# Attention with normalized q and k, then a hard-swish feed-forward: a longer planned time for transposing DMAs and a fourth staging buffer

## The chip, the cores and the metric

The kernel runs on one core of a Trainium2 chip. Such a core has five engines, each of which takes its own list of instructions strictly in order: TensorE (PE in the profile; its weight loads are shown apart as PEld), VectorE (DVE), ScalarE (ACT), GpSimd (POOL) and SyncE (SP). They wait for each other through semaphores. SP here issues nearly all the DMAs; GpSimd issues those that load the weights.

The metric is the time of one execution on the device in microseconds. The kernel before took 441.98 us, the median of three runs (438.52, 443.76 and 441.98).

## What is computed

Eight sequences of 448 rows with 12 heads of 64 go through attention; q and k are normalized by their root mean square first. The output is laid out as 3584 rows of 768 and goes through a feed-forward block with 2048 inner columns.

```python
def rmsnorm(x, g):
    return x / np.sqrt(np.mean(x * x, axis=-1, keepdims=True) + 1e-06) * g
q_n, k_n = rmsnorm(q, g_q), rmsnorm(k, g_k)
scores = np.matmul(q_n, k_n.transpose(0, 1, 3, 2)) / np.sqrt(64)
attn = softmax(scores)                       # over the last axis
x = np.matmul(attn, v).transpose(0, 2, 1, 3).reshape(8 * 448, 768)
h = x @ w_in
out = (h * np.clip(h + 3.0, 0.0, 6.0) / 6.0) @ w_out
```

Inputs and output are float32; the kernel multiplies in bfloat16.

## The kernel before

**Tiling.** Two heads make a pair (`p`, 48 of them counted from 0, six per sequence); two pairs make a group (24), which is the unit of loading. The 448 rows of a head are three tiles of 128 and a rest of 64; the rests of two heads share a tile.

**Steps of a pair.** k, q and v of a group are loaded by SP into one of `NS` staging buffers (`kq_in`, `v_st`: L235, L236; `load_k` L287, `load_q` L278, `load_v` L294). Per pair, GpSimd (early also ScalarE) squares q and k (L334, L332), VectorE sums the squares (L337), ScalarE makes the reciprocal root (L345, L348), and GpSimd multiplies (L353), which gives `qk`, still with rows on the partitions. `qk` is then transposed. For the first 14 pairs (`TD`) TensorE does it (L367), with copies out of its accumulator by VectorE or ScalarE (L385, L388, called at L303). From pair 14 on a transposing DMA on SP does it in one step (`transposes_dma`, L377: 128 rows of 1024 bfloat16), and ScalarE multiplies the q half by the gains afterwards (`scale_q`, L374). Then come the scores on TensorE (L395, for the rests L402), the exponential on ScalarE (L408), the weighting of v on TensorE (L429, L435), and the division on VectorE (L445, L446), which gives `xn`. A second transpose brings `xn` into `xT`: on TensorE for the first 12 pairs (`XD`; L464, L475), after that by another transposing DMA on SP (L468).

**Feed-forward.** For each sequence and each of 16 inner tiles six matmuls (L479) read `xT`; ScalarE and VectorE form the gate (L485, L490) into `gT`; then rows of the output are 16 matmuls of 384 columns each (L498), copied out (L303) and stored by SP (L510). These matmuls fill TensorE between the steps of attention, and about the last 100 us are nothing else.

**What sets the order.** No order is written out by hand. When the program is built, class `Plan` plays it through: each operation has a key (lower goes first), one or several engines with a duration, the operations that it depends on, and a `lag`, the time from the end of its issue to its result. `Plan.run` goes forward in planned time and gives each engine that is free the ready operation with the lowest key. The order in which it hands them out becomes the order of each engine's instructions. On the chip the semaphores see to it that data is there; so a planned time that is too short gives no wrong result, but an instruction that stands in its engine's list before its data has come, with everything behind it waiting too.

For a transposing DMA, `dma_transpose` plans 1270 ns on SP and a lag. Both kinds use it: q and k with `transposes_dma`, `xn` with `x_out_dma` (in `x_stage`). A plain load is planned with 600 ns for each issue on SP and a lag of 1700 ns (`ISSUE`, `LAND`), and all DMAs share one planned pipe of 270 bytes per ns.

**Buffers.** A load into a staging buffer depends on the work that read it before: for k and q the two normalizations of the group `NS` groups earlier, for v its casts. These lines say it (L680, L681); `g` is the group, `norm_g` its normalizations, `vc` the casts of v:

```python
old = norm_g[g - NS] if g >= NS else [clr[g]]
oldv = vc[p - NS * GP:p - NS * GP + GP] if g >= NS else [clv[g]]
```

Each staging buffer is cleared once where the rests leave rows empty (`clear`, `clear_v`: L518 to L524). Other rings keep their sizes: four of `kq`, three of `qk` and `xn`, eight of exponentials, two of squares and of sums.

**Weights.** GpSimd issues the weight loads (L313, L318) between its own work, released in the plan after the v loads of given groups.

Of the kernel before, what the change touches and what calls it, by code (L numbers as in the profile page):

```python
# [63 lines left out]
class Plan:  # L64
# [28 lines left out]
        return op  # L93

    def dma_transpose(self, key, size, fn, deps):
        return self.add(key, [("SP", 1270, fn)], deps, 2100, 1.4 * size)

    def item(self, lane, place, count, ns, fn, deps):

# [89 lines left out]
def kernel(  # L189
# [22 lines left out]
    NFT = DFF // P  # L212
    assert D == 64 and NT == 3 and REST == 64 and DM == H * D and B % 2 == 0

    NS = 3
    GP = 2
    NV, NK, NX, NE, NQ = 4, 4, 3, 8, 3
    YC = 384
# [8 lines left out]
    def ring(n, shape, dtype, name, pool=const):  # L227
        return [pool.tile(shape, dtype, name=f"{name}{i}") for i in range(n)]
# [5 lines left out]
    gprime = const.tile([P, 1], FP32, name="gprime")  # L234
    kq_in = ring(NS, [P, GP, 2, 2, 4, D], FP32, "kq_in")  # L235
    v_st = ring(NS, [P, GP, 2, 4, D], FP32, "v_st")  # L236
    vaug = ring(NV, [P, 4, 2, D + 1], BF16, "vaug")
# [34 lines left out]
    def part_of(p, n):  # L272
        return (p // GP) % NS, slice(p % GP, p % GP + n)

# [30 lines left out]
    def cast(eng, out, in_):  # L305
        if eng is nc.vector:
            eng.tensor_reduce(out=out, in_=in_.unsqueeze(len(in_.shape)), axis=mybir.AxisListType.X, op=A_MAX)
        else:
            copy(eng, out=out, in_=in_)
# [12 lines left out]
    def which(part):  # L322

        return slice(0, 2) if part == 2 else slice(part, part + 1)

    def raw(p, part):
        return kq_in[(p // GP) % NS][:, p % GP, :, which(part)].rearrange("p h a t d -> p h (a t) d")

# [30 lines left out]
    def cast_v(eng, p):  # L359
        out = vaug[p % NV][:, :, :, 0:D].rearrange("p t h d -> p h t d")  # L360
        in_ = v_st[(p // GP) % NS][:, p % GP]
        cast(eng, out, in_)
# [153 lines left out]
    def clear(eng, i):  # L516

        eng.memset(kq_in[i][REST:P, :, 0, 0, NT, :], 0.0)  # L518
        eng.memset(kq_in[i][0:REST, :, 1, 0, NT, :], 0.0)
        eng.memset(kq_in[i][REST:P, :, :, 1, NT, :], 0.0)  # L520

    def clear_v(eng, i):
        eng.memset(v_st[i][REST:P, :, 0, NT, :], 0.0)
        eng.memset(v_st[i][0:REST, :, 1, NT, :], 0.0)  # L524
# [136 lines left out]
    def by(key, pool, dve, fn, deps):  # L661
        return add(key, [("POOL", pool, lambda: fn(G)), ("DVE", dve, lambda: fn(V))], deps)
# [4 lines left out]
    clear_v(V, 0)  # L667
    clr = [by((i * GP - 3, 0), 600, 350, lambda e, i=i: clear(e, i), []) if i else None for i in range(NS)]
    clv = [by((i * GP - 3, 1), 350, 200, lambda e, i=i: clear_v(e, i), []) if i else None for i in range(NS)]
# [168 lines left out]
```

## Time and profile before

| | |
|---|---|
| median of 3 runs | 441.98 us (438.52 to 443.76) |
| the profiled execution | 439.38 us, of which the span in the trace is 437.6 |
| PE busy | 409.8 us, 94% |
| DVE / ACT / POOL busy | 234.7 / 254.3 / 195.2 us |
| DMA | 64.55 MB, 148 GB/s over the span |
| granted TensorE clock | 0.996 of full speed |

The page also gives the busy share in 40 slices of the span, 10.9 us each, in tenths (9 is 90% or more), and the busy share of the 16 DMA engines in the same way:

```profile
PE   0677899999999998999999999999999999999997
ACT  3886887734877885968778587666643032132100
POOL 3697785596377776859676556311000000000000
DMA  6999999995978898999999994333211201100022
```

TensorE is filled after the first five slices up to the end, with one slice at 8 in the middle. The DMA engines are full for most of the first 24 slices, which is where q, k, v and the weights are loaded, and where the transposing DMAs run; GpSimd ends with them. Afterwards only feed-forward work is left.

How such lines are read: in a list of waits, "DVE rden L445 <- PE av L435: 47.1, 45, 3.4" means that VectorE stood idle before its instructions of line 445 (which write `rden`) until TensorE had ended those of line 435, 47.1 us in sum, 45 times, 3.4 at the longest. In a timeline the columns are start, duration, engine, line, operation, out<-in with shapes, count, and in brackets the idle time before it with what ended it. A matmul's bar is longer than the time by which it holds up the next one, since matmuls are pipelined.

### The profile page before, as it was taken

Reading aid. Unit: us, or ns where it says so; the run is one execution under the profiler, and the core shown is the slowest. Engines: PE = TensorE matmul, PEld = TensorE weight load, DVE = VectorE, ACT = ScalarE, POOL = GpSimd, SP = SyncE. Lnnn points to the kernel's source line nnn. Section 1 sums busy time; section 2 is a strip of 40 time slices with the busy share of each in tenths; the row PEclk is TensorE's granted clock in tenths of the full one; section 3 lists DMA queues with packets and bytes.
Section 4 is the critical chain, followed back from the end, with each engine's and each line's share of the span. In section 5 each row is a group of like instructions: output and inputs, shape, how many; then the busy total and the mean of one; then the engine's idle time right before and its main releaser. Section 6 shows DMA issues by size and latency. Waiting matters only on the chain.

```text
span 437.6 us, 8944 instructions
## 1 busy us (share of the span) xinstructions
PE 409.8 (94%) x3520; PEld 236.5 (54%) x3520; DVE 234.7 (54%) x492; ACT 254.3 (58%) x414; POOL 195.2 (45%) x146
## 2 busy tenths in 40 slices
PE   0677899999999998999999999999999999999997
PEld 0355565555566554555555555555565555555565
DVE  6486777766455557556466366344444253343322
ACT  3886887734877885968778587666643032132100
POOL 3697785596377776859676556311000000000000
PEclk9998999999999999999999999999999999999999
DMA  6999999995978898999999994333211201100022
GB/s 170 267 228 216 221 222 239 250 190 131 237 161 190 204 217 189 201 219 194 227 212 167 191 213 121 73 88 91 61 24 49 72 1 51 59 36 37 25 85 73
DMA packets 126506, 64.55 MB, mean 148 GB/s; under 512 B 77824, under 2 KB 123008, under 8 KB 126464
## 3 DMA queue, kind: packets, MB, share of 16 engines
q1 hardware_dynamic: 117488, 57.24, 57.5%
q0 software_dynamic: 8144, 6.29, 9.2%
q8 instruction: 27, 0.44, 0.4%
q10 hardware_dynamic: 832, 0.46, 0.4%
q14 instruction: 15, 0.12, 0.1%
HBM read 45.61 MB, written 11.01 MB: 129 GB/s over the span
## 4 chain that ended last, share of the span: by engine, by line
PE 82%; DMA 7%; ACT 3%; DVE 3%; SPq 2%; POOL 2%; issue 1%; ACTq 0%; POOLq 0%
PE m L479 18%; PE m L498 17%; PE t_ps L498 9%; PE t_ps L479 8%; PE av L435 7%; PE sc L395 6%; PE sc L498 6%; PE sc L479 4%; DMA kq_in<-in_k_dram 3%; DMA kq<-qk 3%; PE av L429 2%; DMA kq_in<-in_q_dram 2%; PE sc L402 2%; ACT eT L408 2%; DVE ssq L337 1%
## 5 line engine op out<-in xcount | busy, mean ns | idle before, releaser
L408 ACT ACTIVATE eT<-sc 128x896 bf16<-128x896 f32 x168 | 147.2, 915 | 42.2 <-PE sc L395 38.5
L498 PEld LDWEIGHTS <-gT 128*128 128x128 bf16 x912 | 85.5, 98 | 61.7 <-issue 8.9
L479 PE MATMUL m<-xT,w_in_sb 128*128 128x448 bf16 x486 | 109.9, 353 | 1.7 <-DVE xT L475 0.6
L479 PEld LDWEIGHTS <-w_in_sb 128*128 128x128 bf16 x768 | 70.7, 98 | 68.8 <-issue 12.0
L353 POOL TENSOR_TENSOR qk<-kq_in,rstd 128x1024 bf16<-128x1024 f32 x47 | 89.0, 1903 | 41.6 <-DMA kq<-qk 20.8
L498 PE MATMUL m<-w_out_sb,gT 128*128 128x384 bf16 (+1 forms) x480 | 87.3, 324 | 0.0
L334 POOL TENSOR_TENSOR sq<-kq_in 128x1024 f32<-128x1024 f32 x41 | 77.2, 1894 | 13.0 <-DMA kq_in<-in_q_dram 3.6
L490 DVE SCALAR_TENSOR_TENSOR gT<-t_sb,m 128x448 bf16<-128x448 f32 x81 | 49.9, 618 | 41.8 <-ACT t_sb L485 41.4
L485 ACT ACTIVATE t_sb<-m 128x448 f32<-128x448 f32 x81 | 44.1, 546 | 47.9 <-PE m L479 47.2
L337 DVE TENSOR_REDUCE ssq<-sq 128x16 f32<-128x1024 f32 (+1 forms) x49 | 58.1, 1190 | 9.5 <-POOL sq L334 7.5
L435 PE MATMUL av<-vaug,eT 128*128 128x65 bf16 x1152 | 59.6, 196 | 0.0
L435 PEld LDWEIGHTS <-eT 128*128 128x128 bf16 x1152 | 52.8, 100 | 7.2 <-issue 1.6
L498 PE MATMUL t_ps<-w_out_sb,gT 128*128 128x384 bf16 x256 | 46.9, 326 | 0.0
L395 PE MATMUL sc<-kq 64*128 64x448 bf16 x288 | 41.6, 363 | 4.0 <-ACT eT L408 2.5
L429 PE MATMUL av<-vaug,eT 128*128 128x130 bf16 x192 | 43.0, 224 | 2.4 <-ACT eT L408 1.2
L479 PE MATMUL t_ps<-xT,w_in_sb 128*128 128x448 bf16 x192 | 44.5, 352 | 0.7 <-DVE gT L490 0.7
L303 POOL CAST vaug<-v_st 128x512 bf16<-128x512 f32 x33 | 20.3, 620 | 55.0 <-PE av L435 46.6
L445 DVE RECIPROCAL rden<-av 128x4 f32<-128x4 f32 x96 | 17.3, 180 | 48.8 <-PE av L435 47.1
L446 DVE TENSOR_TENSOR xn<-av,rden 128x256 bf16<-128x256 f32 x96 | 40.7, 424 | 3.3
L374 ACT ACTIVATE kq<-kq,gprime 128x448 bf16<-128x448 bf16 x34 | 22.8, 670 | 14.2 <-DMA kq<-qk 14.2
L498 PE MATMUL sc<-w_out_sb,gT 128*128 128x384 bf16 (+1 forms) x176 | 29.1, 319 | 0.0
L485 ACT ACTIVATE t_sb<-t_ps 128x448 f32<-128x448 f32 x32 | 17.5, 547 | 19.7 <-PE t_ps L479 18.5
(50 smaller groups left out, 225.0 us busy)
## 6 DMA issues: line engine op xcount, KB each, us to landing
v_st<-in_v_dram SPq DMA_DIRECT2D x24, 384.0 KB, 4.7
kq_in<-in_k_dram SPq DMA_DIRECT2D x23, 384.0 KB, 4.5
kq_in<-in_q_dram SPq DMA_DIRECT2D x23, 384.0 KB, 4.8
out_dram<-y_sb SPq DMA_DIRECT2D x23, 384.0 KB, 2.6
w_out_sb<-in_moe_w_out_dram POOLq DMA_DIRECT2D x4, 768.0 KB, 19.1
w_in_sb<-in_moe_w_in_dram POOLq DMA_DIRECT2D x3, 768.0 KB, 16.2
out_dram<-y_sb SPq DMA_DIRECT2D x9, 192.0 KB, 2.7
v_st<-in_v_dram SPq DMA_DIRECT2D x48, 32.0 KB, 4.3
```

Of the source, the lines that this page charges most:

```text
L334: eng.tensor_tensor(out=sq, in0=x, in1=x, op=A_MULT)
L337: nc.vector.tensor_reduce(out=ssq_r[(p // GP) % 2][:, p % GP, :, which(part)].rearrange("p h a t -> p h (a t)"), in_=sq_r[m][:, :, which(p ...
L353: eng.tensor_tensor(out=qk_r[p % NQ][:].rearrange("p a t h d -> p h (a t) d"), in0=raw(p, 2), in1=rstd_r[(p // GP) % 2][:, p % GP].rearran ...
L395: nc.tensor.matmul(out=sc[:, h, 0:S], lhsT=kT_r[p % NK][rows, t * P:(t + 1) * P], rhs=qT_r[p % NK][rows], start=True, stop=True,)
L408: nc.scalar.activation(out=e2_r[d % NE][:, :, 0:S], in_=sc_r[i][:, :, 0:S], func=EXP, bias=0.0, scale=1.0,)
L429: nc.tensor.matmul(out=av, lhsT=rest[:, cols], rhs=va[:, 3].rearrange("p h d -> p (h d)"), start=True, stop=False, skip_group_check=True,)
L435: nc.tensor.matmul(out=av[:, h * W:(h + 1) * W], lhsT=e[t][h][:, cols], rhs=va[:, t, h], start=False, stop=(t == NT - 1 and h == 1), skip_ ...
L446: nc.vector.tensor_tensor(out=xn_r[p % NQ][:, t].rearrange("p n (h d) -> p n h d", h=2), in0=av4[:, :, :, 0:D], in1=rden.unsqueeze(3).to_b ...
L479: nc.tensor.matmul(out=m[:, 0:S], lhsT=w_in_sb[:, kt, f * P:(f + 1) * P], rhs=xT[:, kt, b % NX, x_slot(b)], start=(kt == 0), stop=(kt == N ...
L485: nc.scalar.activation(out=t[:], in_=m[:, 0:S], func=RELU, bias=0.5, scale=1.0 / 6.0,)
L490: nc.vector.scalar_tensor_tensor(out=gT[:, f, (b % 2) * S:(b % 2 + 1) * S], in0=t[:], scalar=1.0, in1=m[:, 0:S], op0=A_MIN, op1=A_MULT,)
L498: nc.tensor.matmul(out=m[:, 0:n], lhsT=gT[:, f, c0:c0 + P], rhs=w_out_sb[:, f, c:c + n], start=(f == 0), stop=(f == NFT - 1),)
```

## The change

Two numbers change. The lag of both kinds of transposing DMAs in the plan goes from 2100 to 3500 ns; the planned time on SP stays at 1270. The number of staging buffers for groups goes from three to four, for `kq_in` and for `v_st`.

```diff
     def dma_transpose(self, key, size, fn, deps):
-        return self.add(key, [("SP", 1270, fn)], deps, 2100, 1.4 * size)
+        return self.add(key, [("SP", 1270, fn)], deps, 3500, 1.4 * size)
```

```diff
-    NS = 3
+    NS = 4
     GP = 2
```

No operation is computed differently. There are five more clears for the fourth buffer. Because both numbers enter the plan, the order of instructions changes on every engine, and some operations that may run on several engines (casts, copies, squares) go to another one.

## The prediction

> **What bounds the kernel now.** I read four views in this order: busy time by stretch of the span, the chain of waits (for the pace of TensorE), who waited for whom, and the timelines of ScalarE and TensorE around the longest of those waits.
>
> ```profile
> core 0: us, PE busy (x) PEld busy (x) DVE busy (x) ACT busy (x) POOL busy (x), PEclk, DMA share, GB/s
> 20.00:60.00 40.00, 33.64 (x401) 21.72 (x400) 29.98 (x70) 31.35 (x50) 33.87 (x26) 0.96 1.13 224
> 60.00:150.00 90.00, 89.94 (x820) 52.02 (x819) 56.67 (x113) 60.95 (x101) 61.39 (x40) 1.00 0.94 201
> 150.00:240.00 90.00, 85.91 (x806) 48.52 (x804) 57.26 (x112) 69.13 (x117) 64.48 (x41) 1.00 0.97 203
> 240.00:310.00 70.00, 70.00 (x646) 39.18 (x644) 34.11 (x77) 49.55 (x77) 25.56 (x19) 1.00 0.62 127
> ```
>
> TensorE (PE) is the bound: outside the start its bars fill every stretch but 150 to 240, where 4.1 us are open. A bar is longer than a matmul's share of PE, so open time is understated. The pace comes from the chain of waits:
>
> ```profile
> 377.26 2.60 PE m L498 x16
> 382.46 1.13 PE t_ps L479 x6
> 154.83 0.48 PE sc L395 x4
> 155.80 0.06 PE av L429
> 155.86 0.19 PE av L435 x6
> ```
>
> That is 0.1625 us for L498, 0.189 for L479 (and L402, as wide), 0.12 for L395, 0.06 for L429 and 0.032 for L435 (the small transposes L367 and L464, by the same view, 0.055). With the counts of matmuls by line, the work in 150 to 240 is 141 x 0.1625 + 175 x 0.189 + 14 x 0.189 + 84 x 0.12 + 56 x 0.06 + 336 x 0.032 = 82.8 us, so 7.2 us of 90 went unused. The same sum leaves 1.9 unused in 60 to 150, 1.3 in 240 to 310, 0.9 after 310, 13.3 in 20 to 60 and 17.3 in 0 to 20. All work is the same after the change, so only these can shrink or grow. What stands behind the 7.2:
>
> ```profile
> ACT kq L374 <- DMA kq<-qk: 14.2, 11, 2.8
> PE sc L402 <- ACT eT L408: 2.0, 3, 0.9
> PE sc L395 <- ACT eT L408: 1.5, 2, 1.0
> PE t_ps L479 <- DVE gT L490: 0.7, 1, 0.7
> ```
>
> ```profile
> 170.23 0.67 ACT L374 ACTIVATE kq<-kq,gprime 128x448 bf16<-128x448 bf16 x1 [2.82 <-DMA kq<-qk]
> 170.80 1.71 ACT L408 ACTIVATE eT<-sc 128x896 bf16<-128x896 f32 x2
> 171.75 0.36 PE L395 MATMUL sc<-kq 64*128 64x448 bf16 x2 [1.04 <-ACT eT L408]
> 175.80 0.54 PE L402 MATMUL sc<-kq 128*128 128x448 bf16 x2 [0.76 <-ACT eT L408]
> ```
>
> ScalarE takes its work in the planned order. The planner puts the scaling of q (L374) where it believes the transposing DMA (L377) to be done, 1.27 + 2.1 = 3.37 us after its issue begins. The DMA is later, ScalarE stands 2.82 us, and the exponentials queued behind it (L408, of the pairs before) come late; they hold the score buffers, so PE stands at the next scores. How late the DMA is (issue to landing, in 150 to 250 us):
>
> ```profile
> DMA to landing us min/median/max: 3.1/4.1/6.0
> ```
>
> **The change, part by part.**
>
> *The longer planned time.* Planned landing goes from 3.37 to 4.77 us after issue; no instruction is added. The eleven waits of L374 are 0.81, 2.82, 0.95, 1.12, 1.30, 1.47, 0.41, 1.98, 1.77, 0.91 and 0.62 us. With 1.4 us taken off each, 1.42 + 0.07 + 0.58 + 0.37 = 2.4 of 14.2 are left, so 83% go. The new order agrees: between a scaling and the first exponential of its own scores there stood 4.4 exponentials on average, now 3.3, and for pairs 22 to 29 (scores from about 155 to 200 us) two to five fewer. One exponential is 0.915 us, so the shift is about the 1.4 us. Of the 7.2 us unused I leave 1.9 as the floor that the 90 us before show; 5.3 are stalls, 4.4 of them the five waits for L408 (3.5 idle, and about 0.16 each under the tail of a bar, 0.353 long against 0.189) and 0.9 the gate (L490). Gain: 4.4 x 0.83 = 3.7 us.
>
> Is something else late next? What is placed later on ScalarE is also later on PE: from the eighth group of heads on, scores stand 2 to 5 us of PE work later in the new order (78.5 to 82.7 us of work ahead of them, at the end 276.2 to 280.4), with feed-forward matmuls drawn ahead in their place. The last 100 us of PE work are the same in both orders. Attention ends later with no cost while the first feed-forward matmul of the last batch (at 312.3 us of PE work in both) still finds its input: the last weighting ends at 296.8, and division, transposing DMA and landing take about 0.6 + 4.7 us from their longest rows, so 10 us of cover remain; without it each us would cost one.
>
> By the Trainium skill, page "DMA: Bandwidth & Descriptors", section "Anatomy of one DMA — SWDGE (gpsimd) path", a DMA is about 2.0 us and bytes over 436 GB/s; for the 262 KB of this one that makes an estimated 2.6 us, the old plan would already be long enough and this term zero. The trace disagrees (3.1 at the least, 4.1 median), so the row decides.
>
> *The fourth staging buffer.* It lets loads run further ahead on SP's queue. Counted in the order, the load of a group's k stood 3 to 5 pairs ahead of its own transpose from the eleventh to the sixteenth group, now 6; squares on GpSimd (L334) stood 0 to 2 pairs ahead of their normalization, now mostly 3. That removes the 0.9 us of the gate: the chain there goes back over ssq and sq (161.16) to a load of k that took 3.50 us from 157.09. SP issues as many transfers as before, the loads about one group earlier; so the first transposing DMA of q and k (91.25 us now) has one more group's k and q ahead of it. These two loads take about 4 us (0.92 MB at 224 GB/s); the scores behind that DMA start at 108.5 now and 4.2 us of work later then, so 10 us of cover stay.
>
> *The start.* PE's order is the same up to 12 us of work (36.4 us of span). The fifth group's k and q now go ahead of its v: 0.46 MB less ahead of them. ScalarE waits 0.74 us for that q (square at 32.11) and PE stands 0.53 us on the exponential behind it: gain 0.7. On GpSimd the squares of the sixth group move ahead of the fifth group's normalization:
>
> ```profile
> 44.98 3.76 POOL L353 TENSOR_TENSOR qk<-kq_in,rstd 128x1024 bf16<-128x1024 f32 x2 [0.45 <-ACT rstd L348]
> 48.70 3.74 POOL L334 TENSOR_TENSOR sq<-kq_in 128x1024 f32<-128x1024 f32 x2
> 55.62 3.76 POOL L353 TENSOR_TENSOR qk<-kq_in,rstd 128x1024 bf16<-128x1024 f32 x2
> ```
>
> GpSimd is free for them from 39.1 (a square from 37.25); the second needs a sum that VectorE ends at 42.58, so it ends at 44.5, and the normalization at 44.98 starts no later. The next one can then follow at 50.2 instead of 55.62, and its transpose stands 5.9 us of work earlier on PE (28.9 to 23.0; PE is at 23.0 at 52.42): just in time. The gate that waited for the sum of the square at 48.70 (0.5 us idle on PE and 0.1 under a bar) comes free: gain 0.6. From below: all this fails if the sixth group's k and q land late. They are issued by 34.9 and used at 48.70; 1.9 us earlier, they land between 37.8 (median landing 4.8) and 46.8. At the late end the squares end at 50.6, the normalization waits from 44.98 to 50.6, and PE loses 5.6. Earlier loads of the first four groups keep their order, so nothing better than 3 us is in reach (the gaps over 0.3 us from 30 to 50 sum to 5). I take 1.3, near the early end: the fifth group's q, issued by 28.5, was used at 32.11, so a load there took less than the median.
>
> *Five more clears* on VectorE, ahead of its first sum (starts 6.29; the clears end at 5.42 and five take 1.1 more): 0.3 us late, hidden behind the q load that lands at 13.9; 0.3 without that cover. Casts move between engines (VectorE three rows more, ScalarE four fewer), all under 80% busy: nothing.
>
> Sum: 3.7 + 0.9 + 1.3 = 5.9 us. The profiled execution took 439.38 (span 437.6 and 1.8 around it): 433.5. Against the median of 441.98 it is 2.6 short, so on the median 436.1; I say 436.
>
> **The rivals.**
> 1. *The start pays it back.* The late end above: minus 4.6, plus 5.6, 443. For it, the DMA share is 1.13 there and SP takes 4.77 us over one load from 36.97; against it, the order of issue. 15%.
> 2. *The reckoning was not what held ScalarE*, so waits only move: the landing is 3.1 where ScalarE waits and something else comes last. Only gate and start are left, 2.2 us: 440. The skill's fit above would give this. Eleven waits ending at the landing speak against it. 8%.
> 3. *Slower: transposes land later still.* Deeper loads on the same queue stand ahead of each transpose, and in the new order 9 of 34 scalings stand with no exponential between them and their own scores, against 3. Waits of 14.2 cost 5.3 us, 0.37 each. A median landing m costs 34 x (m - 4.77) x 0.37: from m = 5.2 it eats the 5.3, and at 6.0, the longest of that stretch, it is 15.5, so 441.98 + 10 = 452. For it: a DMA share of 0.97 from 150 to 240. By the same page, section "Queues, rings and completion order", each DMA engine takes descriptors in ring order; no row here shows a ring. Against it: the bytes are the same, and loads and transposes alternate as before. 14%.
> 4. *The start gains its 3 us too:* 434. 8%.
>
> **How the numbers follow.** The forecast has 55%; its own range is 433 to 440 (the runs differ by 5.2 us). About 1% (4.4 us) is what a measurement can tell from no change. Below 437.6: 44 of the forecast's 55 and rival 4's 8, 0.52. Slower: rival 3, 0.14. Within: the rest, 0.34. The range of 8 in 10 goes from 431 (434 and the profiled run's 2.6 below the median) to 443 (rival 1); rival 3 lies outside.
>
> **What would show it.** L374's wait for the transpose under 4 us in sum, and 150 to 240 with over 89 us of PE busy: the first step. Squares of the sixth group ending by 45 and the third normalization row near 50: the start. The landing's median under 4.8: not rival 3. It is wrong if L374's waits go and PE's open time stays, or if PE waits at 47 to 53 us for GpSimd's qk.

## The result and the profile after

The changed kernel takes 443.14 us (median of 20 runs, 441.33 to 446.31) against 440.05 for the kernel before on the same chip (20 runs, 437.43 to 444.09): a ratio of 1.0081, 95% interval 1.0063 to 1.0098. It became 3 us slower where 6 us of gain were forecast, and lies just above the range given (431 to 443). Its profiled execution took 443.62 us with a span of 441.8, against 439.38 and 437.6. The ratios in this document leave out three slow runs (one of the kernel with v loads on GpSimd, two of the one with the late landing planned).

TensorE's time by stretch, as for the kernel before (the first two numbers of a row are the stretch and its length, then the busy time of PE, PEld, DVE, ACT and POOL with counts, the granted clock, the DMA share and GB/s):

```profile
20.00:60.00 40.00, 32.28 (x386) 20.92 (x384) 29.34 (x67) 27.99 (x45) 33.81 (x23) 0.91 1.18 231
60.00:150.00 90.00, 89.01 (x797) 51.37 (x796) 57.55 (x114) 60.14 (x98) 56.04 (x38) 1.00 0.91 198
150.00:240.00 90.00, 86.46 (x806) 47.70 (x806) 55.87 (x112) 68.94 (x114) 64.51 (x43) 1.00 1.04 202
```

The start lost 1.4 us of busy time (33.64 before) at a lower granted clock (0.91, 0.96 before), and 150 to 240 is as open as it was (85.91 before, both with 806 matmuls). The list of waits says the same of the wait that the longer planned time was to shrink from 14.2 us:

```profile
ACT kq L374 <- DMA kq<-qk: 13.9, 10, 3.1
```

To compare the same work rather than the same time, I use one sum throughout: the start of a matmul, less the time by which the matmuls ahead of it occupy PE at the prediction's paces. That is the time that PE has left unused by then; where the granted clock is low, what PE loses by it counts as unused too.

| us of PE work done | 12 | 16 | 20 | 28 | 40 | 130 | 140 | 240 | 310 |
|---|---|---|---|---|---|---|---|---|---|
| unused, before | 26.2 | 28.5 | 30.0 | 30.8 | 31.5 | 33.3 | 37.2 | 41.6 | 42.7 |
| unused, after | 25.1 | 27.0 | 31.3 | 34.5 | 35.1 | 37.1 | 37.5 | 45.8 | 46.9 |

So there are three steps. Up to 16 us of work the new kernel is 1.5 us ahead. It then loses 5 us, in two stalls and in a stretch at half the clock, and is 3.6 behind at 40. At 130 to 140 (about 163 to 177 us of the span before) the old kernel loses 3.9 us and the new one 0.4: there the old stalls did go. But from 140 to 240 it loses 8.3 where the old one lost 4.3. Nothing happens afterwards, and the 4.2 at the end is the difference of the spans.

**The two stalls of the start.** From the timelines of GpSimd, VectorE, ScalarE and TensorE of the changed kernel:

```profile
41.55 3.74 POOL L334 TENSOR_TENSOR sq<-kq_in 128x1024 f32<-128x1024 f32 x2 [1.49 <-DVE rden L445]
45.25 3.76 POOL L353 TENSOR_TENSOR qk<-kq_in,rstd 128x1024 bf16<-128x1024 f32 x2
...
43.47 1.22 DVE L337 TENSOR_REDUCE ssq<-sq 128x16 f32<-128x1024 f32 x1 [1.61 <-POOL sq L334]
...
45.30 0.28 PE L464 MATMUL m<-identity,xn 128*128 128x128 bf16 x2 [1.68 <-DVE xn L446]
...
58.44 1.06 ACT L332 ACTIVATE sq<-kq_in 128x1024 f32<-128x1024 f32 x1 [3.42 <-issue]
...
60.63 0.35 PE L479 MATMUL m<-xT,w_in_sb 128*128 128x448 bf16 x1 [2.08 <-DVE gT L490]
```

First stall: GpSimd takes the squares of the sixth group at 41.55, ahead of the normalization, as the prediction said. Its wait is put down to VectorE, whose instruction had ended at 41.40; the load of that group's q, issued until 32.11, landed at 41.34. VectorE's list holds the sum of that square (L337) ahead of a division that was ready (L446, at 44.82). It stands 1.61 us, and TensorE then waits 1.68 us for the quotient. Behind this stall TensorE runs at a lower clock. The stretch from 40 to 50 us, in the kernel before and in the changed one:

```profile
40.00:50.00 10.00, 8.03 (x106) 5.16 (x105) 6.70 (x18) 8.22 (x13) 6.54 (x6) 1.00 1.19 224
40.00:50.00 10.00, 7.47 (x87) 4.74 (x87) 7.44 (x16) 5.45 (x9) 8.51 (x7) 0.83 1.19 223
```

Over 46.5 to 50 us the granted clock is 0.51 in the changed kernel and 1.00 in the one before; 3.4 us at half the clock cost an estimated 1.7 us of PE's time. Both kernels have one such stretch earlier (from 35.2 us before, from 29.5 in the changed one), so this one is extra. Whether the stall brought it on was not tried.

Second stall: a square of the seventh group stands in ScalarE's list (L332); in the kernel before both squares of that group were GpSimd's, at 59.90. ScalarE idles 3.42 us for it. The chain of waits names the load (with 12.19 us, up to an exponential that ran meanwhile):

```profile
42.01 12.19 DMA kq_in<-in_q_dram
...
59.96 0.62 DVE gT L490
```

That q was issued from 42.01 to 45.52 and landed at 58.29, 16.3 us after its issue began. Behind the square stood the gate (L485) and so gT and the feed-forward matmuls. The kernel before issued the same q at almost the same time:

```profile
42.74 3.44 SPq L282 DMA_DIRECT2D kq_in<-in_q_dram  x1
```

There too it landed 16.3 us later, at 59.1, and its squares followed at 59.90. So the load did not become slower, and hardly earlier; what moved is the place of its square in the lists. The list of DMA queues for 28 to 62 us says with whom the load shared the engines (packets, MB, share of the 16 engines' time):

```profile
q0 software_dynamic: 4951, 3.93, 73.4%
q1 hardware_dynamic: 6405, 3.61, 46.1%
```

The first is GpSimd's, the weights. By the Trainium skill, page "DMA: Bandwidth & Descriptors", section "Anatomy of one DMA — SWDGE (gpsimd) path", whose fit is for DMAs that GpSimd issues, a 384 KB load alone would be an estimated 2.0 + 0.9 = 2.9 us; SP issued these, and their medians here are 8.8 for q and 12.7 for k. The plan's own terms for such a load are a lag of 1.7 us and 1.5 us of its pipe.

**The stalls from 140 us of work on.** SP's, GpSimd's and ScalarE's timelines around the longest wait:

```profile
201.53 3.76 POOL L353 TENSOR_TENSOR qk<-kq_in,rstd 128x1024 bf16<-128x1024 f32 x2
...
208.24 1.26 SPq L292 DMA_DIRECT2D kq_in<-in_k_dram  x2
209.60 1.64 SPq L468 DMA_TRANSPOSE xT<-xn  x1
211.33 1.39 SPq L377 DMA_TRANSPOSE kq<-qk  x1
...
214.89 0.67 ACT L374 ACTIVATE kq<-kq,gprime 128x448 bf16<-128x448 bf16 x1 [3.09 <-DMA kq<-qk]
```

The first `qk` of that row is ready at 203.43. SP issues its transposing DMA at 211.33, 7.9 us later; it lands 3.54 us after that, and ScalarE has waited 3.09. SP hardly waits in between: one issue follows another with 0.04 to 0.1 us of pause (the profile puts 1.4 us of L468's 1.64 down to VectorE, but others of L468 take 1.24 with no wait, so about 0.4 of the 7.9 can be that). From 180 to 210 us 27.7 of its 30 us are issues, with the waits that lie inside them, and 0.3 separate semaphore instructions; in the kernel before 27.4 and 0.3. The delay from a ready `qk` to its issue is mostly 5 to 17 us over pairs 20 to 47 in both kernels (below 5 us at five of these pairs before and one after), and the time from landing to use, 18 us at pair 14 in the new kernel and 11 in the old, has drained to nothing by pair 28 in the new one and 24 in the old. The plan reckons 600 ns for an issue of a load and 1270 for a transposing DMA; with the pauses they are about 680 and 1430.

Part of such a delay is planned. `Plan` sets a start for every operation when the program is built; the table has the start in the trace less the planned one, in us, for the transposing DMA of a pair's q and k on SP and for its scaling on ScalarE. A value that stays the same along a row says only that the two count from different zeros or that time was lost in the start.

| pair | 17 | 21 | 25 | 29 | 35 |
|---|---|---|---|---|---|
| before, SP's issue | 1.9 | 3.7 | 8.0 | 7.0 | 9.5 |
| before, scaling | 2.9 | 2.6 | 2.7 | 6.1 | 9.6 |
| after, SP's issue | 6.1 | 8.4 | 13.2 | 15.6 | 14.7 |
| after, scaling | 6.8 | 6.7 | 6.4 | 9.2 | 12.3 |

SP slips first, by 6 to 8 us, while ScalarE still keeps its distance from the plan; when the lead of the landings is used up (pair 26 before, 28 after), ScalarE starts to wait and slips with it.

So the theories to test were two. **Queue (Q):** SP runs later and later against its plan, and L374 waits for a late issue rather than for a long landing. **Start (S):** the plan believes the early loads to land long before they do; with three buffers the planned wait for a buffer held them, and the work that reads them, back in the plan, and with four that work stands in VectorE's and ScalarE's lists ahead of work that is ready.

### The profile page after: what moved, and what is told of

It reads as the page before. It is cut to its first block, busy times and chain, and to the rows that moved or that the text cites. A ratio compares the mean times of both kernels' runs of the same rounds, so it can differ in the third digit from the quotient of the medians.

```text
span 441.8 us, 8954 instructions
## 1 busy us (share of the span) xinstructions
PE 411.4 (93%) x3520; PEld 236.0 (53%) x3520; DVE 237.3 (54%) x500; ACT 252.9 (57%) x410; POOL 194.2 (44%) x147
## 4 chain that ended last, share of the span: by engine, by line
PE 75%; DMA 10%; SPq 4%; ACT 4%; DVE 3%; issue 2%; POOL 2%; ACTq 0%; POOLq 0%
PE m L498 18%; PE m L479 16%; PE t_ps L479 8%; PE t_ps L498 7%; PE sc L498 6%; PE av L435 6%; DMA kq_in<-in_q_dram 6%; PE sc L395 5%; PE sc L479 4%; PE av L429 2%; ACT eT L408 2%; DMA kq<-qk 2%; SPq L292 2%; PE sc L402 2%; DVE gT L490 1%
## 5 line engine op out<-in xcount | busy, mean ns | idle before, releaser
L479 PE MATMUL m<-xT,w_in_sb 128*128 128x448 bf16 x462 | 105.7, 353 | 4.1 <-DVE gT L490 2.7
L498 PE MATMUL m<-w_out_sb,gT 128*128 128x384 bf16 x544 | 99.6, 326 | 0.0
L334 POOL TENSOR_TENSOR sq<-kq_in 128x1024 f32<-128x1024 f32 x40 | 75.3, 1893 | 31.8 <-DVE ssq L337 14.9
L490 DVE SCALAR_TENSOR_TENSOR gT<-t_sb,m 128x448 bf16<-128x448 f32 x77 | 47.5, 617 | 37.4 <-ACT t_sb L485 36.9
L485 ACT ACTIVATE t_sb<-m 128x448 f32<-128x448 f32 x77 | 41.9, 544 | 39.3 <-PE m L479 38.1
L337 DVE TENSOR_REDUCE ssq<-sq 128x16 f32<-128x1024 f32 (+1 forms) x49 | 57.8, 1188 | 7.6 <-POOL sq L334 6.8
L479 PE MATMUL t_ps<-xT,w_in_sb 128*128 128x448 bf16 x222 | 51.0, 353 | 0.0
L446 DVE TENSOR_TENSOR xn<-av,rden 128x256 bf16<-128x256 f32 x96 | 40.7, 424 | 3.3
L485 ACT ACTIVATE t_sb<-t_ps 128x448 f32<-128x448 f32 x37 | 20.2, 546 | 29.1 <-PE t_ps L479 28.5
L498 PE MATMUL t_ps<-w_out_sb,gT 128*128 128x384 bf16 (+1 forms) x192 | 34.7, 320 | 0.0
L303 DVE COPY y_sb<-m 128x384 f32<-128x384 f32 x29 | 16.1, 556 | 31.6 <-PE m L498 31.4
L490 DVE SCALAR_TENSOR_TENSOR gT<-t_sb,t_ps 128x448 bf16<-128x448 f32 x37 | 22.9, 618 | 18.1 <-ACT t_sb L485 18.0
```

Source lines behind the costliest of these rows:

```text
L334: eng.tensor_tensor(out=sq, in0=x, in1=x, op=A_MULT)
L337: nc.vector.tensor_reduce(out=ssq_r[(p // GP) % 2][:, p % GP, :, which(part)].rearrange("p h a t -> p h (a t)"), in_=sq_r[m][:, :, which(p ...
L446: nc.vector.tensor_tensor(out=xn_r[p % NQ][:, t].rearrange("p n (h d) -> p n h d", h=2), in0=av4[:, :, :, 0:D], in1=rden.unsqueeze(3).to_b ...
L479: nc.tensor.matmul(out=m[:, 0:S], lhsT=w_in_sb[:, kt, f * P:(f + 1) * P], rhs=xT[:, kt, b % NX, x_slot(b)], start=(kt == 0), stop=(kt == N ...
L485: nc.scalar.activation(out=t[:], in_=m[:, 0:S], func=RELU, bias=0.5, scale=1.0 / 6.0,)
L490: nc.vector.scalar_tensor_tensor(out=gT[:, f, (b % 2) * S:(b % 2 + 1) * S], in0=t[:], scalar=1.0, in1=m[:, 0:S], op0=A_MIN, op1=A_MULT,)
```

## The experiments

All were timed in five rounds against the kernel before on the same chip. "Start" is PE's unused time by 40 us of work, "middle" what is added from 130 to 240 (31.5 and 8.2 before, 35.1 and 8.7 after), "L374" the scaling's wait for transposing DMAs (14.2 before, 13.9 after).

| kernel | us | ratio to before, 95% interval | start | middle | L374 |
|---|---|---|---|---|---|
| lag 3500 alone | 436.35 | 0.9966 (0.9941 to 0.9992) | 31.5 | 6.6 | 6.9 |
| four buffers alone | 445.37 | 1.0175 (1.0146 to 1.0204) | 37.1 | 8.2 | 9.2 |
| changed, squares kept on GpSimd | 441.14 | 1.0079 (1.0051 to 1.0107) | 36.7 | 6.7 | 7.3 |
| before, 28 more issues on SP | 449.23 | 1.0261 (1.0236 to 1.0287) | 30.3 | 16.4 | 27.5 |
| lag, q loads on ScalarE's queue | 452.65 | 1.0321 (1.0293 to 1.0348) | 49.3 | 3.0 | 0.4 |
| lag, v loads on GpSimd's queue | 438.68 | 0.9997 (0.9968 to 1.0027) | 32.8 | 4.3 | 4.2 |
| lag, true issue times planned | 435.01 | 0.9920 (0.9897 to 0.9942) | 30.9 | 3.1 | 4.2 |
| old lag, true issue times planned | 437.94 | 0.9995 (0.9975 to 1.0015) | 31.1 | 8.6 | 14.1 |
| changed, early loads held | 434.40 | 0.9911 (0.9887 to 0.9935) | 30.2 | 4.1 | 4.8 |
| changed, early loads held, true issue times | 434.45 | 0.9937 (0.9907 to 0.9967) | 30.4 | 4.2 | 4.8 |
| changed, late landing planned | 437.67 | 0.9975 (0.9946 to 1.0004) | 29.4 | 9.2 | 5.8 |
| changed, late landing and true issue times | 433.04 | 0.9888 (0.9862 to 0.9913) | 29.8 | 2.9 | 2.5 |

The last three columns are of one profiled execution each, and the clock enters them. In these traces it falls to half for 3.4 us at a time, or for a multiple of that. In the first 70 us that is 3.4 us in the kernel before, 6.8 in the changed one, 10.2 with four buffers alone and with the squares kept on GpSimd, none with more issues, with the old lag and true issue times and with the late landing planned; in the middle it is 3.4 us in those last two and with four buffers alone, and none in the others. So 1 to 3 us between two rows can be the clock.

**Each half alone.** The kernel before with the lag of 3500:

```diff
-        return self.add(key, [("SP", 1270, fn)], deps, 2100, 1.4 * size)
+        return self.add(key, [("SP", 1270, fn)], deps, 3500, 1.4 * size)
```

> The longer planned time alone, three staging buffers. Theory Q (in the loading phase SP issues back to back, so a transposing DMA is late because SP comes to it late, not because it lands late; a longer planned time only moves the place of ScalarE's scaling once, and the lead is used up again): the waits of L374 for the transposes stay at 8 us or more in sum, and the time is within 1.5 us of before. The prediction's theory (each wait shrinks by 1.4 us): waits of 2 to 4 us in sum and 3.7 us less than before. The start, which the order of the first 60 us leaves as before, loses nothing by either.

and with the fourth buffer:

```diff
-    NS = 3
+    NS = 4
```

> The fourth staging buffer alone, old planned time. Theory S (with the fourth buffer the plan sets squares and their sums of the sixth and seventh group ahead of loads that have not landed, and VectorE and ScalarE stand with TensorE's work behind them): PE has lost about 3.5 us more than before by 60 us of work, in two stalls near 43 and 58 us, and the time is 3 to 4.5 us over before. Rival (the loss of the start comes from the five clears and from chance): under 1 us more than before by 60 us of work.

The lag alone gains 1.8 us on the median and leaves 6.9 us of waits: less than the prediction's theory asked, and a little more than Q allowed. The buffer alone loses 7.2, more than the 3 to 4.5 expected, and 5.6 of it in the start (up to an estimated 3.4 of them by 6.8 us more at half the clock). The loss is the buffer's, and most of it lies where the prediction had hoped for 1.3 us of gain.

**The squares of the seventh group on GpSimd.** The changed kernel, with ScalarE offered the squares of six groups only:

```diff
-    NFAST = 8
+    NFAST = 6
```

> The changed kernel with ScalarE allowed to square only for the first six groups (NFAST 6), so the square of the seventh group that it waited 3.4 us for goes back to GpSimd. Theory S: the stall near 58 us (2.2 us on PE) goes, the one near 43 stays; 2 to 2.5 us less than the changed kernel, still 0 to 2 over before. Rival (the late q of the seventh group holds TensorE wherever the square stands): no more than 0.5 us off the changed kernel.

```profile
PE m L479 <- DVE gT L490: 3.4, 1, 3.4
```

This line of its waits from 40 to 70 us shows the stall in a new place: by 28 us of work the start is repaired (30.2 unused, 34.5 in the changed kernel), by 40 it is at 36.7. The ratio to before is that of the changed kernel (1.0079 and 1.0081), so ScalarE's square as such was not the cause: the rival held, and the 2 to 2.5 us of gain that S had expected did not come. The profiled execution took 443.53 us, where the median is 441.14, with the clock at half for 6.8 us from 64.3, so its 36.7 may overstate the usual loss. As long as a square of a late q is ordered early, on whichever of the two engines, TensorE pays.

**More issues, the same bytes.** The kernel before, with the loads of v's rests (L300) as one DMA for each head from the eleventh group on, 28 more instructions on SP; the order on the other engines stays as it was:

```diff
-            eng.dma_start(out=st[rows, :, h, NT, :], in_=rest)
+            for i in range(n) if p >= 20 else ():
+                eng.dma_start(out=st[rows, i, h, NT, :], in_=rest[:, i])
+            if p < 20:
+                eng.dma_start(out=st[rows, :, h, NT, :], in_=rest)
```

> The kernel before, with each of the two loads of v's rests cut in two from the eleventh group on: 28 more issues on SP, the same bytes, the same planned order of everything else. Theory Q: each costs SP about 0.66 us, 1.3 us a group; about seven groups are loaded while SP is full, so the time grows by 5 to 9 us and L374's waits for the transposes double at least. Rival L (the transposes are late because the 16 DMA engines are shared): the bytes are the same, so the time stays within 1.5 us of before.

The list of waits (here the transposing DMA is L380, the scaling L377) and the stretch from 150 to 240:

```profile
ACT kq L377 <- DMA kq<-qk: 27.5, 13, 3.5
```

```profile
150.00:240.00 90.00, 79.00 (x740) 44.29 (x737) 51.67 (x102) 63.16 (x106) 59.37 (x38) 1.00 0.83 193
```

The 28 issues cost 11.1 us (449.23 against 438.13), 0.40 each and above the 5 to 9 expected, and the waits nearly doubled, while the DMA share in that stretch fell from 0.97 to 0.83 and the median from issue to landing of these DMAs, 150 to 250 us, from 4.1 to 3.3. It is SP's queue that the scalings wait for, not the DMA engines' bandwidth: Q. The Trainium skill, page "DMA: Bandwidth & Descriptors", section "Issuing engines are not separate DMA queues", calls the time to start a DMA "usually small relative to the DMA itself"; for one load of this stretch the trace agrees (0.6 us of 3.5 to 4.0 to its landing, medians), but in sum SP does little else.

**Taking load off SP.** With the lag of 3500, the q loads from the ninth group on issued by ScalarE:

```diff
-                eng, queue = (nc.scalar, "ACT") if g < QA else (nc.sync, "SP")
+                eng, queue = (nc.scalar, "ACT") if g < QA or g >= 8 else (nc.sync, "SP")
```

> Three buffers and the longer planned time, with the loads of q from the ninth group on issued by ScalarE's queue instead of SP's: two issues, about 1.3 us a group, fewer on SP, the same bytes. Theory Q: PE's lost time between 130 and 230 us of work falls by 3 us or more against the longer planned time alone (8.7 to 10 us lost after 40 us of work there), and the time by 2 to 5 us. Rival L (shared DMA engines, landing times): nothing falls; ScalarE's own 1.3 us a group cost 0 to 3 us.

ScalarE's timeline:

```profile
60.20 0.54 ACT L485 ACTIVATE t_sb<-m 128x448 f32<-128x448 f32 x1
73.56 0.44 ACTq L281 DMA_DIRECT2D kq_in<-in_q_dram  x1
...
77.86 0.92 ACT L408 ACTIVATE eT<-sc 128x896 bf16<-128x896 f32 x1 [17.12 <-DMA kq_in<-in_q_dram]
```

The profile ends this wait with the landing of another load of q, one that SP had issued at 63.87; the last reader of the buffer had ended by 59.40, so the buffer was free. On ScalarE's list the exponentials wait with the load, 17.1 us here. In the middle 0.4 us of waits for transposing DMAs are left and PE lost 3.0 us instead of 8.2; from pair 30 to 37 SP issues 0.6 to 5.4 us after a ready `qk`, against 8.1 to 18.8 with the lag alone. That fits Q, but at a price of 18 us in the start, so the 2 to 5 us of gain that Q had forecast did not come, and a stall of that size changes much besides. The v loads on GpSimd, which has idle time there:

```diff
-            lv_g[p] = plan.dma((p if g else VL, 2), 3, GP * kb, lambda p=p: load_v(nc.sync, p, GP), oldv)
+            veng, vqueue = (nc.gpsimd, "POOL") if g >= 8 else (nc.sync, "SP")
+            lv_g[p] = plan.dma((p if g else VL, 2), 3, GP * kb, lambda p=p, veng=veng: load_v(veng, p, GP), oldv, queue=vqueue)
```

> Three buffers and the longer planned time, with the loads of v from the ninth group on issued by GpSimd: three issues, about 2 us a group, fewer on SP, 0.9 us each on GpSimd, the same bytes. Theory Q: L374's waits for the transposes fall from 6.9 to under 3 us and the time by 2 to 5 us against the longer planned time alone. Rival L: the waits stay, and GpSimd's 2.7 us a group make the time 0 to 4 us longer.

Its middle improves to 4.3 and the waits fall to 4.2 (under 3 expected by Q), but the runs counted spread from 434.45 to 440.52, and the time is not told apart from the kernel before, where Q had it 2 to 5 us under the lag alone. It decides nothing.

**SP's true times in the plan.** With the lag of 3500; no instruction is added:

```diff
-        op = self.add(key, [(queue, self.ISSUE[queue] * n, fn)], deps, self.LAND, size, hold)
+        ns = 680 if queue == "SP" and key[0] >= 16 else self.ISSUE[queue]
+        op = self.add(key, [(queue, ns * n, fn)], deps, self.LAND, size, hold)
...
-        return self.add(key, [("SP", 1270, fn)], deps, 2100, 1.4 * size)
+        return self.add(key, [("SP", 1430, fn)], deps, 3500, 1.4 * size)
```

> Three buffers and the longer planned time, with SP's planned costs set to what the trace shows with the pause behind each: 680 ns for an issue of a load from the ninth group on (was 600), 1430 for a transpose (was 1270). Nothing else is told to the plan. If SP falls behind its plan group by group (theory Q), the plan now sees it, puts feed-forward work where TensorE stood, and the time falls by 1 to 4 us against the longer planned time alone; if the plan is off because of landing times, within 1 us of it.

and the same with the old lag of 2100:

> The kernel before (three buffers, lag 2100) with SP's true times in the plan (680 ns for a load issue from the ninth group on, 1430 for a transposing DMA); with the lag of 3500 the same gave 435.01 us against 438.13 before. If the late SP was the whole of the old waits and the landing itself was of no account, the lag does nothing and this gives the same, 434.5 to 436. If the planned landing was too short as well (1.43 + 2.1 = 3.53 us against a landing of 4.1 in the median), L374 still waits here, about half of the 14.2 us in 150 to 240 us, and the time is 436.5 to 438.5.

(The kernel before took 438.53 in the set of the 435.01.) The two corrections do more together. From the middle of 8.2 us the lag alone takes 1.6, the issue times alone nothing (an estimated 1.5 of its 8.6 is the half clock), both together 5.1. In time the surplus over the two alone is 1.8 us, which these intervals barely tell from none. A sum fits it: a transposing DMA's result is late by SP's delay and by its own landing, 4.1 us in the median from the start of its issue, where a lag of 2100 makes 3.4 to 3.5. Correct one and ScalarE still stands for the other. That the old lag leaves the waits whole (14.1) was in neither theory; half was expected.

**Holding the early loads.** The changed kernel, with the loads of the first ten groups waiting as with three buffers:

```diff
-            old = norm_g[g - NS] if g >= NS else [clr[g]]
-            oldv = vc[p - NS * GP:p - NS * GP + GP] if g >= NS else [clv[g]]
+            W3 = 3 if g < 10 else NS
+            old = norm_g[g - W3] if g >= W3 else [clr[g]]
+            oldv = vc[p - W3 * GP:p - W3 * GP + GP] if g >= W3 else [clv[g]]
+            if g == 3:
+                old, oldv = [*old, clr[g]], [*oldv, clv[g]]
```

> The changed kernel with the loads of the first ten groups held in plan and on the chip as if there were three buffers; from the eleventh group on four are used. Clears and memory are those of the changed kernel, and the order of the first 60 us of TensorE's work is that of before. Theory S: the start loses what it lost before (about 31.5 us at 40 us of work, not 35 to 37), and the time is 3.5 to 5 us under the changed kernel, at or under the one with the longer planned time alone. Rival (clears, memory or later loads cost the start): still 34 or more at 40 us of work.

With this the start is that of before and better (30.2 unused), and the kernel beats the changed one by more than the 3.5 to 5 us expected (0.9911 against 1.0081). The fourth buffer is harmless once the start is past; with it and the lag the middle falls to 4.1, 2.5 less than with the lag alone. Adding SP's true times gave nothing more:

> The changed kernel with both repairs that each gave a part: the loads of the first ten groups held as with three buffers (434.40 us alone), and SP's instructions planned with the times that the trace shows, 680 ns for each load issue from the ninth group on and 1430 for a transposing DMA (435.01 us alone, with three buffers). The theory that SP runs late against its plan says that the waits of L374 left in 150 to 240 us (4.8 us with the first repair) shrink under 3, with 150 to 240 filled to 89.5 us or more: 432 to 434.5 us. The rival, that a deep fourth buffer already gives SP all the slack that it can use, says no gain over the first repair alone, 434 to 435.5.

Its rival held: 434.45, with the same 4.8 us of waits.

**What the plan believes of the landing.** Holding a load also changes when it runs. This kernel changes a belief only: the loads of the sixth to eighth group are planned to land 11 us later, and nothing waits for more than in the changed kernel:

```diff
-        op = self.add(key, [(queue, self.ISSUE[queue] * n, fn)], deps, self.LAND, size, hold)
+        late = 11000 if queue == "SP" and 10 <= key[0] < 16 else 0
+        op = self.add(key, [(queue, self.ISSUE[queue] * n, fn)], deps, self.LAND + late, size, hold)
```

> The changed kernel (four buffers, lag 3500), with one number of the plan made true: the loads of the sixth to eighth group on SP's queue are planned to land 11 us later than before, about what the trace shows for q there (12.19 us from issue). No buffer and no wait is added. The theory that the start is lost because the plan believes those loads to be there long before they are, and so stands their squares in GpSimd's and ScalarE's lists ahead of work that is ready, says: 31 to 33 us unused on PE by 40 us of its work (35.1 in the changed kernel, 31.5 in the one before) and 439 to 441 us. The rival, that it is the earlier loads themselves that hold each other up, whatever the plan believes of them, says 34 us or more unused by then, and 442 to 445.

The start falls to 29.4, below the 31.5 of before and the 31 to 33 expected: S, and not the loads' own contention (the seventh group's q still lands 14.6 us after an issue at 43.4; this execution has no half-clock stretch in the start, but the last kernel of the table has one and reaches 29.8). The time too is below the 439 to 441 expected. In the middle one large wait remains, and it shows Q in one piece (SP, ScalarE and TensorE; lines after 91 are one higher here):

```profile
186.53 1.31 SPq L378 DMA_TRANSPOSE kq<-qk  x1
...
192.60 0.67 ACT L375 ACTIVATE kq<-kq,gprime 128x448 bf16<-128x448 bf16 x1 [4.92 <-DMA kq<-qk]
...
194.13 0.23 PE L430 MATMUL av<-vaug,eT 128*128 128x130 bf16 x1 [3.88 <-ACT eT L409]
```

The `qk` of that DMA was ready at 173.48. Against the plan it was issued 6.7 us late, and ScalarE, 1.1 us late at the scaling before, was 6.2 late at the one that waits for it. Both corrections together, four buffers and the lag of 3500 as in the change:

> The changed kernel (four buffers, lag 3500) with two corrections in the plan alone: the loads of the sixth to eighth group planned to land 11 us later, and SP's instructions planned with the times of the trace (680 ns for a load issue from the ninth group on, 1430 for a transposing DMA). With the first alone the start was repaired (29.35 us unused on PE by 40 us of its work, 31.5 before) and one wait of L374 of 4.92 us, for a transposing DMA that SP issued 13.05 us after its qk was there, cost 5.7 us at 187 to 194 us. The theory that SP is late against its plan says that this wait goes: no single wait of L374 over 2.5 us in 150 to 240 us, and 430.5 to 434 us. The rival, that the fourth buffer brings such a wait whatever the plan believes of SP, says 435.5 to 438.

```profile
20.00:60.00 40.00, 34.85 (x432) 22.47 (x431) 31.95 (x74) 33.45 (x52) 33.55 (x24) 0.96 1.13 231
60.00:150.00 90.00, 89.91 (x812) 52.26 (x811) 58.75 (x116) 57.99 (x96) 58.16 (x38) 1.00 1.05 209
150.00:240.00 90.00, 90.00 (x836) 50.99 (x834) 56.69 (x112) 71.49 (x117) 65.24 (x42) 1.00 0.99 210
```

The stretches are filled; 150 to 240 takes 836 matmuls where before and after had 806. At 433.04 us it beats the kernel before by 4.8 us and the changed kernel with it, and it differs from the latter in planned numbers alone. SP is now 0.1 us off its plan at pair 17 and 4.7 at pair 35, ScalarE between 0.3 and 2.3 late from pair 17 on, and no wait of the scaling is over 1.1 us. One rival no run here excludes: a plan changed as much without being made truer, since a changed order may win or lose some us by chance. Against it stand the forecasts that held for the time (the lag with true issue times, this kernel) and the slips above.

## Why the prediction was wrong

*The longer planned time (3.7 us forecast): cause incomplete, gain not there.* "The DMA is later" was read from issue to landing, and that part was right: the longer lag is needed (437.94 without it, 435.01 with it, each with true issue times). What was missing is the time ahead of the issue. The step took 1.4 us off each old wait as if SP would issue where the plan has it; SP had already slipped against it, from 1.9 us at pair 17 to 8.0 at pair 25. In the changed kernel the old stalls at 130 to 140 us of work did go (3.9 to 0.4 us), and new ones of the same kind came from 140 to 240 (4.3 to 8.3). Alone, the lag gained 1.8 us and left 6.9 us of waits, not 2.4. The prediction's mark for this, waits under 4 us, failed at 13.9. The sum had a smaller fault as well: its 14.2 us of waits are those of 150 to 310 us, and 10.9 of them lie in 150 to 240, whose unused time it set them against. The prediction had asked whether something "is placed later" on ScalarE and PE, but not whether SP keeps to its plan; its timeline in the profile of before would have shown it.

*The fourth buffer (0.9 us): not found alone.* With the buffer alone the middle is 8.2 us, as before (an estimated 1.7 of it the half clock). With the lag it shows: held back early, the buffer takes the middle from 6.6 to 4.1. It is not the gate that the step named: TensorE's wait for it (0.7 us) is gone with the lag alone. From 150 to 250 us TensorE waits 1.6 us for `xn` and 1.4 for exponentials with the lag alone, 0.2 and 0.6 with the buffer held back early.

*The start (1.3 us): the sign was wrong.* The number of its first half held: 1.1 us ahead by 12 us of work and 1.5 by 16, against 0.7 forecast. The cause is not shown: ScalarE still waits 0.36 us at that square, for k (0.74 before, for q), and the half-clock stretch lies elsewhere in the new kernel. GpSimd's part nearly held: squares ending at 45.25 (forecast 44.5), the normalization at 45.25 (44.98), the next at 51.46 (50.2). The step stopped at GpSimd. It priced the squares and not what follows each of them, the sum on VectorE, which now stood ahead of a ready division; and it put the moves between engines at "nothing" by their busy shares, while one of them was a square on ScalarE whose q landed 16.3 us after issue. A busy share says nothing about a move of an instruction whose data is late. The lower clock behind the first stall, an estimated 1.7 us, was in no term. The landing of 4.8 us, a median over the whole kernel, was the wrong row for a time in which weights held 73% of the engines.

*Five clears (0):* no cost was seen beyond 0.2 us at PE's first matmul (9.55 against 9.38).

*Rival 1, the start pays it back (443):* right in place, sign and total, but for another reason, so that the total is right is luck. It had the sixth group's normalization wait until 50.6; that did not happen. The losses were VectorE's sum and ScalarE's square. Its 443 also counted the 3.7 us of the first step and the 0.9 of the second as gained, and they were not.

*Rival 2, waits only move (440):* its core is what the middle did, though not because the landing was reckoned wrongly: the lag and the issue were both short. *Rival 3, later landing:* no. The median from 150 to 250 us is 4.0 (4.1 before). *Rival 4* fell with the start.

With the early loads held the same two numbers gain 4.1 us (434.40 against 438.53) of the 5.9 forecast: the start is what turned the sign.

## What to carry to other kernels

Where a planner orders the instructions, compare its planned time of every queue with the trace, the one that only issues DMAs included: such an engine shows no busy time, so its lateness appears as waits for DMAs elsewhere. A lag that repairs a wait works in full only if the issue is on time as well. An extra buffer removes a planned wait that may have been keeping wrong estimates harmless; before adding it, set the true landing of what it releases, or hold it back where the landing is longest.

## What the runs showed of the hardware

SP's issues take time when nothing waits: 0.53 to 0.65 us for a load and about 1.25 to 1.45 for a transposing DMA, with 0.04 to 0.1 us between; 28 more of them without a byte more cost 11.1 us. While the weights load, an issue itself stretches (L292 at 36.32 took 3.78 us), and a q of the seventh group lands 16.3 us after its issue began, in the kernel before as in the changed one. The granted clock fell to half for 3.4 us or a multiple of it in most of these traces. Why an issue stretches there and what lowers the clock were not tried, nor was an order in which the weights come later.
